# First activation loads of the second stage: issued by GpSimd in five consecutive slots in place of SyncE, pools exchanged two slots earlier

## The chip, the cores and the metric

The kernel runs on one core of a Trainium2 chip. Its time is the device time of one execution in microseconds (us), as the median of several runs. The engines are TensorE (PE, with its weight loads as PEld), VectorE (DVE), ScalarE (ACT), GpSimd (POOL) and SyncE (SP, which only issues DMAs); 16 DMA engines move data between HBM and the on-chip memory.

## The reference

Three parts follow each other, all in float32:

```
a    = softmax(phi over s)                    # B=8, H=8, S=576, D=64, 32 memory slots
k_m, v_m = a^T k, a^T v                       # per batch and head
attn = softmax(q k_m^T / 8) v_m               # -> x: 4608 tokens x 512
x = (h * sigmoid(1.702 h)) @ w_out            # h = x @ w_in, 512 -> 2048 -> 512
x = (h * sigmoid(h)) @ w_out2                 # h = x @ w_in2, the same sizes
```

## The kernel before

Each matmul operand is held as a high part in fp32r and the rest, and a product is three passes (high x high, high x rest, rest x high). The work has three stretches that matter here.

**First stage** (to about 350 us): attention and the first layer's h with its silu. It is a row of N1 = 128 slots. In each, `first` (L372, run twice, u = 0 and 1) makes two blocks of h, 12 matmuls in all (L382), in four PSUM banks that go round, and ACT writes the silu of each (L384) into one half of a tile g. Then `store` (L386) sends the tile, 288 KB, to the scratch tensors g1s in HBM. A tile is named here by its slot, 1 to 128. `g_tile` (L366) gives its buffer: four go round under the tag g, and from tile 117 on, two of three tiles take the buffers raw and wst1, of which there is one each:

```
        if n > TAIL and n % 3:
            return moe.tile([128, 2, HS], F32, tag=("", "raw", "wst1")[n % 3], name="g")
```

Tiles 118, 121, 124 and 127 thus share raw, and 119, 122, 125 and 128 share wst1. Raw belonged to a piece of the first layer's second weight matrix before, which is stored to w1t (L434).

**Second stage** (`middle`, 350 to 700 us): the product of g1s with the first layer's second weights, by Strassen's scheme with seven products of blocks. Its activations come back from g1s by `b_fetch` (L726): 128x2x384 floats, 384 KB, a DMA; a call makes one DMA (tiles named r, in the pool xst) or two (both halves of a tile named rr, in the pool xp). `b_prep` (L751) makes the matmul operand op from such a tile: ACT casts it (L759), DVE takes the rest (L455). `b_prod` (L774) runs 12 matmuls (L780) on it. The first eight loads (the first five entries of the list BF) feed the first eight operands; the other eight of the first block, and twelve loads of weights from w1t, are issued by SyncE at the start of `middle`.

**What sets the order.** The first stage's order is written out: `put(x, fn, ...)` books a step at place x, with three places in a slot (two halves of `first`, one `store`), and a loop runs them in order; every engine then executes its own instructions in that order. SyncE issues every DMA, stores and loads alike, one after the other: an issue that waits holds up all behind it. `swap_pools` (L1025) gives back the memory of the attention (pool att and its PSUM banks) and opens xst and xp in it, from which the loads take their tiles. The first operands are made by `b_make`, booked in slots N1 - 3 and N1 - 2 (operands 0 and 1) and at the start of `middle` (2 and 3).

Of the kernel before, what the change touches and what calls it, by code (L numbers as in the profile page):

```python
# [21 lines left out]
def attn_moe_moe(ctx: ExitStack, tc: tile.TileContext, q, k, v, phi, w1i, w1o, w2i, w2o, out):  # L22
    nc = tc.nc
# [28 lines left out]
    g1s = [dram.tile([128, 2, NT], F32, name=f"g1s{f}") for f in range(NP)]  # L52
# [388 lines left out]
    HB = 384  # L441
# [281 lines left out]
    rb, ob, eb = {}, {}, {}  # L723
    TB = HB // 128

    def b_fetch(b, q, p):  # L726


        if q == 2 or (q == 0 and p < 2):
            x = p if q else 5 + p  # L730
            ts = {p: pools["xst"].tile([128, 2, HB], F32, tag=f"xr{x}", name="r")}
        else:
            i = {0: (0, 6), 1: (5, 7), 3: (3, 4)}[q][p // 2]
            t = pools["xp"].tile([128, 2, 2, HB], F32, tag=f"x{i}", name="rr")
            ts = {p + n: t[:, n] for n in range(2)}
        c0 = (2 * b + q // 2) * HB
        for p, t in ts.items():
            rb[b, q, p] = t
            nc.sync.dma_start(out=t, in_=g1s[4 * (q % 2) + p][:, :, c0:c0 + HB])

    def b_fetch_after(b, i, p):

        for q in {3: (0, 1), 7: (2,), 4: (3,)}.get(i, ()):
            if q == 2 or (q == 0 and p < 2):
                b_fetch(b, q, p)
            elif p % 2:
                b_fetch(b, q, p - 1)
# [118 lines left out]
    def put(x, fn, *a):  # L866

        todo.setdefault(x, []).append((fn, a))
# [11 lines left out]
    def plan_attention(b, z):  # L880
# [29 lines left out]
        for c in range(4):  # L910
            for x, fn, a in zip(t["wp"][c], (wp_mm, wp_hi, wp_lo), ((), (COPY[t["on"][2][c]],), ())):
# [14 lines left out]
                q=(-37, -37, -36, -34, -29, -28), qe=(-37, -34, -34, -29, -29, -28),  # L926
# [5 lines left out]
                q=(-49, -43, -42, -36, -36, -32), qe=(-43, -39, -32, -34, -34, -32),  # L932
# [5 lines left out]
                q=(-43, -41, -40, -37, -36, -32), qe=(-40, -40, -35, -33, -30, -30),  # L938
# [5 lines left out]
                q=(-42, -41, -41, -40, -36, -36), qe=(-42, -40, -36, -33, -31, -31),  # L944
# [75 lines left out]
            for x, fn in zip(WO["sum"][n], (wo1_sum, wo1_hi, wo1_lo, wo1_tail)):  # L1020
                put(66 + 66 * c + x, fn, c, n)
    N1 = 2 * B * NP
    ZS = N1 - 12

    def swap_pools():  # L1025
        att.release()
# [4 lines left out]

    put(3 * ZS + 2, swap_pools)
    BF = [(0, 0), (0, 1), (0, 2), (1, 0), (1, 2), (2, 0), (3, 0), (2, 1), (2, 2), (3, 2), (2, 3)]
    for n, z in enumerate((1, 3, 5, 7, 9)):
        put(3 * (ZS + z) + 2, b_fetch, 0, *BF[n])
    seqb = [(b, i, p) for b in range(NBK) for i in ORDER for p in range(4)]
    AHEAD = 3
    SUMS = {5: ((0, 0),), 6: ((0, 1), (1, 0), (1, 1)), 7: ((2, 0),), 8: ((2, 1), (3, 0)), 9: ((3, 1),)}
# [208 lines left out]
```

## Time and profile before

| | |
|---|---|
| time, median of 3 runs | 1408.13 us (1405.4 to 1409.28) |
| the profiled execution: its own time | 1412.43 us |
| its span | 1410.6 us |
| TensorE busy | 1377.0 us, 98% |
| VectorE, ScalarE, GpSimd busy | 71%, 57%, 22% |
| mean granted clock of TensorE | 0.996 |

The span runs from the first to the last instruction of the profiled execution; its own time has 1.8 us around it. Busy shares are over the whole span, so they say nothing on a single stretch: what a change at one place is worth is read from the rows of that place. A DMA's issue (SyncE, written SPq) is short; how long the transfer then takes is its landing time, listed apart.

### The profile page before, as it was taken

Reading aid. Unit: us, or ns where it says so; the run is one execution under the profiler, and the core shown is the slowest. Engines: PE = TensorE matmul, PEld = TensorE weight load, DVE = VectorE, ACT = ScalarE, POOL = GpSimd, SP = SyncE. Lnnn points to the kernel's source line nnn. Section 1 sums busy time; section 2 is a strip of 40 time slices with the busy share of each in tenths; the row PEclk is TensorE's granted clock in tenths of the full one; section 3 lists DMA queues with packets and bytes.
Section 4 is the critical chain, followed back from the end, with each engine's and each line's share of the span. In section 5 each row is a group of like instructions: output and inputs, shape, how many; then the busy total and the mean of one; then the engine's idle time right before and its main releaser. Section 6 shows DMA issues by size and latency. Waiting matters only on the chain.

```text
span 1410.6 us, 25823 instructions
## 1 busy us (share of the span) xinstructions
PE 1377.0 (98%) x10058; PEld 1322.9 (94%) x10058; DVE 1003.3 (71%) x1328; ACT 797.5 (57%) x1353; POOL 308.1 (22%) x213
## 2 busy tenths in 40 slices
PE   6899999999999999999999999999999999999998
PEld 4687888788999999999999999999999999999998
DVE  6776676663887778888876344343669988898886
ACT  3767777675454555555566566565775444444442
POOL 1524655642000111200000010010000405135050
PEclk9999999999999999999999999999999999999999
DMA  9797888768965572653355664645574643716531
GB/s 360 241 293 243 296 274 299 264 213 260 340 239 165 182 255 93 239 175 127 112 164 190 202 214 154 210 160 196 181 238 140 191 131 105 210 42 185 138 98 34
DMA packets 217722, 276.95 MB, mean 196 GB/s; under 512 B 50688, under 2 KB 198144, under 8 KB 217600
## 3 DMA queue, kind: packets, MB, share of 16 engines
q1 hardware_dynamic: 217600, 275.31, 59.7%
q8 instruction: 79, 1.29, 0.4%
q14 instruction: 43, 0.35, 0.1%
HBM read 166.20 MB, written 109.05 MB: 195 GB/s over the span
## 4 chain that ended last, share of the span: by engine, by line
PE 92%; ACT 2%; DVE 1%; DMA 1%; issue 0%; POOL 0%; DVEq 0%; ACTq 0%; POOLq 0%
PE pb L780 25%; PE p L679 25%; PE xb L564 14%; PE h L382 13%; PE y L564 11%; PE a L334 2%; PE a L247 1%; PE a L208 1%; DMA phi<-in_phi_dram 1%; ACT L384 1%; PE a L270 1%; ACT phi L186 0%; DMA g1s<-g 0%; ACT g L384 0%; DVE slab L345 0%
## 5 line engine op out<-in xcount | busy, mean ns | idle before, releaser
L780 PE MATMUL pb<-op,wq 128*128 128x384 f32 x2016 | 350.4, 335 | 0.0
L780 PEld LDWEIGHTS pb<-op,wq 128*128 128x128 f32 x2016 | 349.7, 188 | 0.6 <-DVE op L455 0.6
L679 PE MATMUL p<-op,wq 128*128 128x384 f32 x2016 | 350.1, 335 | 0.0
L679 PEld LDWEIGHTS p<-op,wq 128*128 128x128 f32 x2016 | 349.7, 188 | 0.2 <-DVE op L455 0.2
L455 DVE TENSOR_TENSOR op<-rr,op 128x768 fp32r<-128x768 f32 x204 | 235.0, 1161 | 52.3 <-ACT op L664 26.8
L382 PEld LDWEIGHTS h<-attnT,slab 128*128 128x128 f32 x1536 | 209.1, 189 | 40.9 <-ACT g L384 16.3
L382 PE MATMUL h<-attnT,slab 128*128 128x288 f32 x1536 | 231.6, 303 | 10.2 <-ACT g L384 7.0
L564 PE MATMUL xb<-xq,wq 128*128 128x384 f32 x1152 | 218.2, 338 | 0.0
L564 PEld LDWEIGHTS xb<-xq,wq 128*128 128x128 f32 x1152 | 203.1, 188 | 0.2
L859 POOL TENSOR_TENSOR c<-c 128x512 int32<-128x512 int32 x32 | 51.3, 1603 | 614.5 <-DVE c L857 522.9
L455 DVE TENSOR_TENSOR op<-r,op 128x768 fp32r<-128x768 f32 x132 | 145.5, 1110 | 54.2 <-ACT op L759 41.2
L564 PE MATMUL y<-xq,wq 128*128 128x384 f32 x864 | 167.5, 338 | 0.1
L564 PEld LDWEIGHTS y<-xq,wq 128*128 128x128 f32 x864 | 152.6, 188 | 0.5 <-ACT e L624 0.5
L664 ACT CAST op<-rr 128x768 fp32r<-128x768 f32 x108 | 89.6, 837 | 97.5 <-PE p L679 70.8
L384 ACT ACTIVATE g<-h 128x288 f32<-128x288 f32 x256 | 98.7, 416 | 79.4 <-PE h L382 53.4
L573 ACT ACTIVATE gq<-e 128x384 f32<-128x384 f32 x144 | 75.6, 525 | 103.2 <-DVE e L452 103.0
L759 ACT CAST op<-rr 128x768 fp32r<-128x768 f32 x96 | 80.0, 835 | 70.5 <-PE pb L780 43.6
L452 DVE TENSOR_TENSOR e<-e,y 128x384 f32<-128x384 f32 x96 | 52.8, 553 | 63.2 <-PE y L564 57.0
L759 ACT CAST op<-r 128x768 fp32r<-128x768 f32 x72 | 60.1, 836 | 50.1 <-PE pb L780 39.2
L452 DVE TENSOR_TENSOR e<-e,xb 128x384 f32<-128x384 f32 x48 | 26.5, 553 | 80.0 <-ACT c L852 37.8
L664 ACT CAST op<-r 128x768 fp32r<-128x768 f32 x60 | 50.3, 838 | 56.4 <-PE p L679 45.5
L452 POOL TENSOR_TENSOR r<-r 128x768 f32<-128x768 f32 x10 | 22.6, 2281 | 271.7 <-DMA out_dram<-ox 117.7
(112 smaller groups left out, 1410.9 us busy)
## 6 DMA issues: line engine op xcount, KB each, us to landing
g1s<-g SPq DMA_DIRECT2D x128, 288.0 KB, 4.2
gs<-gq SPq DMA_DIRECT2D x192, 192.0 KB, 1.9
rr<-g1s SPq DMA_DIRECT2D x60, 384.0 KB, 6.7
rr<-gs SPq DMA_DIRECT2D x60, 384.0 KB, 5.0
r<-g1s SPq DMA_DIRECT2D x36, 384.0 KB, 4.2
r<-gs SPq DMA_DIRECT2D x36, 384.0 KB, 5.6
q<-in_q_dram SPq DMA_DIRECT2D x16, 576.0 KB, 5.4
xs<-eb SPq DMA_DIRECT2D x24, 384.0 KB, 4.2
```

Source lines behind the costliest of these rows:

```text
L334: nc.tensor.matmul(out=a[u][j:j + 32], lhsT=st["kvT", b][r, s, 1, 32 * m:32 * m + 32], rhs=w1[r, m, cols(c)], start=True, stop=True)
L382: nc.tensor.matmul(out=h, lhsT=w[:, wi, g, f0:f0 + 128], rhs=x[:, xi, g * HS:(g + 1) * HS], start=(g == 0 and n == 0), stop=(g == 1 and n ...
L384: nc.scalar.activation(out=t[:, u], in_=h, func=ACTF.Silu, scale=1.702)
L452: eng.tensor_tensor(out=out, in0=a, in1=b, op=ALU.add)
L455: eng.tensor_tensor(out=out, in0=a, in1=b, op=ALU.subtract)
L564: nc.tensor.matmul(out=out, lhsT=w[:, s, wi, f0:f0 + 128], rhs=x[:, s, xi], start=(start and s == 0 and k == 0), stop=(s == 1 and k == 2), ...
L573: nc.scalar.activation(out=t, in_=h, func=ACTF.Silu, scale=2.0)
L664: nc.scalar.copy(out=t[:, :, 0], in_=s)
L679: nc.tensor.matmul(out=out[:, d], lhsT=w[:, u, wi, d * 128:(d + 1) * 128], rhs=t[:, u, gi], start=(start and p == 0 and u == 0 and k == 0) ...
L759: nc.scalar.copy(out=t[:, :, 0], in_=s)
L780: nc.tensor.matmul(out=out[:, d, :HB], lhsT=w[:, u, wi, d * 128:(d + 1) * 128], rhs=t[:, u, gi], start=(start and p == 0 and u == 0 and n ...
L859: nc.gpsimd.tensor_tensor(out=i, in0=i, in1=low, op=ALU.add)
```

## The change

Five calls of `b_fetch`, eight DMAs, are booked with nc.gpsimd as issuer, in slots ZS + 1 to ZS + 5 (in place of every second slot from ZS + 1 to ZS + 9), and ZS, the slot of `swap_pools`, is N1 - 14 in place of N1 - 12. Other calls of `b_fetch` keep SyncE.

```
-    def b_fetch(b, q, p):
+    def b_fetch(b, q, p, by=nc.sync):
...
-            nc.sync.dma_start(out=t, in_=g1s[4 * (q % 2) + p][:, :, c0:c0 + HB])
+            by.dma_start(out=t, in_=g1s[4 * (q % 2) + p][:, :, c0:c0 + HB])
...
-    ZS = N1 - 12
+    ZS = N1 - 14
...
-    for n, z in enumerate((1, 3, 5, 7, 9)):
-        put(3 * (ZS + z) + 2, b_fetch, 0, *BF[n])
+    for n, z in enumerate((1, 2, 3, 4, 5)):
+        put(3 * (ZS + z) + 2, b_fetch, 0, *BF[n], nc.gpsimd)
```

On SyncE, at the stores of tiles 116 to 121, before (L388 is a store of g, L739 a load; the number behind g1s is the eighth of the scratch, that behind _ the buffer):

```order
L388 DMA g1s3_87<-g_4837 256x1x288
L388 DMA g1s4_88<-g_4855 256x1x288
L739 DMA r_4901<-g1s0_84 128x2x384
L388 DMA g1s5_89<-g_4884 256x1x288
L388 DMA g1s6_90<-g_4904 256x1x288
L739 DMA r_4940<-g1s1_85 128x2x384
L388 DMA g1s7_91<-g_4922 256x1x288
L388 DMA g1s0_84<-g_4943 256x1x288
L739 DMA rr_4978<-g1s2_86 128x2x384
L739 DMA rr_4978<-g1s3_87 128x2x384
```

Two stores, one call's loads, two stores, and so on to the end of the stage. On SyncE at the end of the stage, now:

```order
L388 DMA g1s5_89<-g_5045 256x1x288
L388 DMA g1s6_90<-g_5066 256x1x288
L388 DMA g1s7_91<-g_5084 256x1x288
L739 DMA r_5114<-g1s0_84 128x2x384
L739 DMA rr_5116<-g1s4_88 128x2x384
L739 DMA rr_5116<-g1s5_89 128x2x384
L739 DMA r_5119<-g1s1_85 128x2x384
```

The stores follow each other up to tile 128, and the first loads on SyncE are those that `middle` issues. On GpSimd, from its last sum over the weights (L455) to its next work in the second stage (L859), now:

```order
L455 TENSOR_TENSOR wq_4812<-wst1_4083,wq_4812 128x2x256
L739 DMA r_4865<-g1s0_84 128x2x384
L739 DMA r_4885<-g1s1_85 128x2x384
L739 DMA rr_4905<-g1s2_86 128x2x384
L739 DMA rr_4905<-g1s3_87 128x2x384
L739 DMA rr_4926<-g1s4_88 128x2x384
L739 DMA rr_4926<-g1s5_89 128x2x384
L739 DMA rr_4948<-g1s6_90 128x2x384
L739 DMA rr_4948<-g1s7_91 128x2x384
L859 TENSOR_TENSOR c2_5411<-c2_5411 128x512 x16
```

The eight loads stand in one row there, between L455 and L859, which followed each other before.

## Rows read from the trace of the kernel before

**Rows 1.** The page: TensorE's part of the engine table, and the chain.

```profile
PE 1377.0 (98%) x10058; PEld 1322.9 (94%) x10058; DVE 1003.3 (71%) x1328; ACT 797.5 (57%) x1353; POOL 308.1 (22%) x213
...
PE 92%; ACT 2%; DVE 1%; DMA 1%; issue 0%; POOL 0%; DVEq 0%; ACTq 0%; POOLq 0%
```

**Rows 2.** Stretches: length, busy us (x instructions) of PE, PEld, DVE, ACT, POOL; clock, DMA share, GB/s.

```profile
328.00:330.00 2.00, 1.98 (x13) 1.58 (x12) 2.00 (x4) 0.82 (x2) 0.03 (x1) 1.00 0.68 242
330.00:340.00 10.00, 10.00 (x76) 10.00 (x76) 0.92 (x1) 4.90 (x13) 0.00 (x0) 1.00 0.84 266
340.00:351.00 11.00, 9.29 (x69) 9.06 (x68) 1.92 (x2) 4.75 (x12) 0.00 (x0) 1.00 1.02 303
351.00:360.00 9.00, 9.00 (x54) 9.00 (x53) 3.74 (x5) 5.78 (x11) 0.00 (x0) 1.00 0.98 329
```

**Rows 3.** Order of time on PE: start, us, work [idle before <- what ended it].

```profile
320.35 1.95 PE L334 MATMUL a<-w,kvT 64*32 64x512 f32 x32
...
347.08 3.46 PE L382 MATMUL h<-attnT,slab 128*128 128x288 f32 x24 [1.71 <-ACT g L384]
350.38 15.81 PE L780 MATMUL pb<-op,wq 128*128 128x384 f32 x88
```

**Rows 4.** Chain that ended last, in order of time: start, us, what.

```profile
340.65 5.86 DMA g1s<-g
```

**Rows 5.** Order of time on ACT, 331 to 360 us.

```profile
331.87 0.41 ACT L384 ACTIVATE g<-h 128x288 f32<-128x288 f32 x1 [0.44 <-PE h L382]
332.62 0.41 ACT L384 ACTIVATE g<-h 128x288 f32<-128x288 f32 x1 [0.34 <-PE h L382]
...
335.81 0.41 ACT L384 ACTIVATE g<-h 128x288 f32<-128x288 f32 x1 [0.39 <-PE h L382]
337.98 1.51 ACT L384 ACTIVATE g<-h 128x288 f32<-128x288 f32 x4 [1.75 <-DMA g1s<-g]
...
342.56 0.71 ACT L384 ACTIVATE g<-h 128x288 f32<-128x288 f32 x2 [1.53 <-DMA g1s<-g]
346.62 0.71 ACT L384 ACTIVATE g<-h 128x288 f32<-128x288 f32 x2 [3.35 <-DMA g1s<-g]
...
359.68 0.83 ACT L759 CAST op<-rr 128x768 fp32r<-128x768 f32 x1
```

**Rows 6.** Order of time on SyncE (issues, merged where equal ones follow each other).

```profile
328.38 0.56 SPq L434 DMA_DIRECT2D w1t<-wq  x1
...
332.07 1.43 SPq L739 DMA_DIRECT2D r<-g1s  x1
333.59 1.58 SPq L388 DMA_DIRECT2D g1s<-g  x2
...
339.32 1.24 SPq L739 DMA_DIRECT2D rr<-g1s  x2
340.65 1.27 SPq L388 DMA_DIRECT2D g1s<-g  x2
```

**Rows 7.** POOL: order of time, and one line of its costliest groups (busy, mean ns).

```profile
326.73 1.30 POOL L455 TENSOR_TENSOR wq<-wst,wq 128x512 fp32r<-128x512 f32 x1 [0.21 <-ACT wq L513]
403.51 1.30 POOL L859 TENSOR_TENSOR c<-c 128x512 int32<-128x512 int32 x1 [75.48 <-DVE c L857]
...
L455 POOL TENSOR_TENSOR rr<-rr 128x768 f32<-128x768 f32 x10 | 25.4, 2560 | 0.0
```

**Rows 8.** Landing (median us): stores 300-330, 330-341; w1t store at 328.38; g1s, 318-352.

```profile
g1s<-g SPq DMA_DIRECT2D x15, 288.0 KB, 2.7
...
g1s<-g SPq DMA_DIRECT2D x6, 288.0 KB, 4.2
...
w1t<-wq SPq DMA_DIRECT2D x1, 512.0 KB, 3.3
...
DMA to landing us min/median/max: 2.5/5.4/6.9
```

**Rows 9.** Order of time on DVE: its first operand of the second stage.

```profile
348.09 0.96 DVE L455 TENSOR_TENSOR op<-r,op 128x768 fp32r<-128x768 f32 x1 [17.17 <-ACT op L759]
```

## The prediction

> **What bounds the kernel now.** I read the page's table of engines and its chain first, then the busy time by stretch around the place of the change, then the order of time on TensorE, ScalarE, SyncE, GpSimd and VectorE there. TensorE (PE) is the bound: 98% busy, and 92% of the chain that ended last lies on it [rows 1]. A change to who issues loads can therefore only pay where PE stands still because of the loads. The stretch table shows how much that is: in 330 to 340 us and from 351 to 360 PE is busy all the time, in 340 to 351 it is busy for 9.29 of 11 us, while the share of the DMA engines goes from 0.84 to 1.02 [rows 2]. PE's own list has one gap there, 1.71 us in front of the last 24 first-stage matmuls, ended by the silu of L384 on ScalarE (ACT) [rows 3]. So **1.71 us, 0.12% of the span, is all that this place has to give**.
>
> Why ACT was late is read from the chain in order of time: a store of g that takes 5.86 us stands between ACT and PE [rows 4]. It stands there because of g_tile (L366): from tile 117 on, two tiles of three use one buffer for each of the tags raw and wst1, so tile n of those cannot be written before the store of tile n - 3 has landed. Counted back from the last store (tile 128), ACT's waits [rows 5] are: tile 121 waits 1.75 us for store 118, tile 124 waits 1.53 for store 121, tile 125 waits 3.35 for store 122. The four h banks in PSUM let PE run two tiles ahead, so only the third of these reaches PE. SyncE's list shows a second cause beside the landing: tile 122 was done at 339.49 (337.98 + 1.51, the last of four silus), but its store was issued at 340.65, behind two of the moved loads that held SyncE from 339.32; tile 118, done at 333.03, was issued at 333.59, behind the first moved load, which took 1.43 us [rows 5, 6].
>
> **The change part by part.** *Eight loads leave SyncE.* Five calls of b_fetch are eight DMAs of 384 KB. No store of this stretch stands behind a load any more, so a store goes out when its second silu ends: 0.56 us earlier for tile 118, 1.16 for tile 122. Nothing new takes the place on SyncE. What follows the last store there, the second batch of loads, starts as soon as that store is issued, so no later than now.
>
> *Eight issues come to GpSimd (POOL).* Its last instruction before them is L455, from 326.73 to 328.03, and its next one starts at 403.51 [rows 7]; for 75 us nothing is queued behind the loads. They wait only for matmuls of the attention that lie before 322.3 (the L334 group ends there [rows 3]), so the first goes out at about 328.0, against 332.07 now. No row shows a DMA issued by POOL. The nearest rows are SyncE's issues of the same loads, 1.43 us for the first and 0.62 each for the two at 339.32 [rows 6], and POOL's own pass over a tile of the same size, 2.56 us [rows 7]. The issues are hidden at both ends: at 2.56 the last one starts at 328.03 + 7 x 2.56 = 345.9; with the longest landing of this stretch, 6.9 us [rows 8], it is there at 352.8, and ACT first reads it at 359.68 [rows 5]. I take SyncE's rows as the nearer ones and cost this at nothing. VectorE (DVE) has work until 330.92 and then none until 348.09 [rows 9].
>
> The Trainium skill (SBUF — State Buffer, section SBUF: two separate sides, the box on DVE blocking DMA) speaks against this part: GpSimd writes the descriptors of its DMAs into SBUF and cannot while VectorE holds the port pair that they share, where DMAs from SyncE are immune. By it a load could lose at most VectorE's busy time; the trace leaves 2.9 us of that at the start and none after, so the sum would stay. No run here shows yet whether the lock acts.
>
> *The transfers move forward and together.* The bytes are the same. Before, eight loads were spread over 332 to 350; now they are asked for from 328 on. The room for them is in 328 to 340, where the DMA share was 0.68 and 0.84, and not in 340 to 351, where it was 1.02 [rows 2]. That is good for the late stores and bad for the early ones. The price goes by the landing time L of a store. After a landing ACT needs 0.11 us (340.65 + 5.86 = 346.51 against 346.62 [rows 4, 5]); I use 0.15. Tile 118 is ready at 333.03. Tile 121 starts at 333.05 + L + 0.15 and lasts 0.72; tile 124 starts L + 0.15 after the store of 121, and its first half takes 0.41. That half is done at 334.5 + 2L. PE needs it for tile 126, whose first matmul would start at 343.75: PE came to rest at 345.37 (347.08 - 1.71 [rows 3]) after finishing tile 126, and one tile takes 1.60 (tiles 118 and 120 end on ACT at 333.03 and 336.22 [rows 5]). So **PE stalls 2 x (L - 4.6) us**, nothing below L = 4.6, and as much as now, 1.71, at L = 5.45. The other chain (119, 122, 125), with tile 119 ready at 334.62, gives 336.1 + 2L against 345.35, the same point.
>
> L is bounded by rows: 2.7 us median with little other traffic, 4.2 in 330 to 341, 5.86 for the store that made the gap, 6.9 the longest [rows 4, 8]. I take 4.2, since the new overlap of stores and loads falls into that stretch, and the traffic taken out of 341 to 351 lies where 5.86 was. One more thing is due early: tile 118 takes over the buffer of the last w1t store, issued at 328.38 and landing in 3.3 us [rows 6, 8], just before the tile's first silu at 331.87 [rows 5]. That store has 512 KB, 1.6 us of data at the 329 GB/s of a full stretch [rows 2]; if loads beside it double that, tile 118 ends at 328.38 + 4.9 + 0.15 + 0.72 = 334.15 in place of 333.03 and puts 1.1 us on the chain. With L = 4.2 the slack is 0.8, so a stall of 0.3 us remains.
>
> *The swap of the pools* two slots earlier leaves the order of the work on PE, ACT and DVE as it is and puts no wait there but those for the loads themselves; it lies behind the last matmul into the released banks and costs nothing.
>
> Sum: -1.71 + 0.3 = **-1.4 us**. Against the profiled execution (1412.43 us, span 1410.6) that is 1411.0; against the median of the runs, 1408.13, it is **1406.7 us**. From 351 to 360 PE has no idle time [rows 2]; the second batch of loads starts no later and finds less queued before it, so I count nothing there.
>
> **The rivals.** *The stores lose to the bunched loads* (the one on the other side). POOL asks for 3.1 MB within eight issues, while a store of 288 KB comes each 1.60 us, on the same DMA engines. If L goes to 6.9 in 333 to 344, the stall is 2 x 2.3 = 4.6 us, 2.9 more than now: 1411.0. It decides from L = 5.45. For it: a store right behind two loads took 5.86 [rows 4], and the w1t store is now hit too. Against it: the loads lie over a stretch with a share of 0.84, stores no longer stand behind them on SyncE, and a late tile delays the next store and so thins the traffic. Between 1408.1 and 1411.0, chance 0.32.
>
> The Trainium skill (DMA: Bandwidth & Descriptors, section Issuing engines are not separate DMA queues) has a rule near this rival: DMAs of all issuers end on the same 16 engines, and a second issuer saves only issue time. By that alone, with each landing as now, tile 125's first half would be done at 339.45 + 5.86 + 0.15 + 0.41 = 345.87, a stall of 0.5 us, and the time 1406.9. The trace agrees in that the DMA share was already 1.02.
>
> *POOL's issues are slow, so that the change doesn't bring the loads early.* Then PE waits for op at L780. The eighth load feeds the eighth product; a product is 12 matmuls, 12 x 15.81/88 = 2.16 us [rows 3], so its operand is due at 350.38 + 7 x 2.16 = 365.5, and its cast and subtraction (0.83 + 0.96 [rows 5, 9]) begin by 363.7. An issue may take (363.7 - 6.9 - 328.03)/7 = 4.1 us before anything is late. At 5 us the load lands at 369.9 and PE loses 6 us: 1414. For it: the trace has no such issue. Against it: the nearby rows are at 2.56 or below, and DVE is idle. Chance 0.06.
>
> *The stall was this execution's own*: the other runs did not have it, and the time stays at 1408.1. For it: there is one profile, and the three runs lie 3.9 us apart. Against it: the waits follow from buffers and sizes that are the same each time. Chance 0.10.
>
> **How the numbers follow.** The forecast, L below 5, has 0.52. Its likeliest time is 1406.7, and its own range is 1404.4 (a gain of all 1.71 less half of the spread of the runs) to 1407.5 (a stall of 1.1 us). The range for 8 in 10 takes in the rival of the bunched loads and the same spread below: 1403.8 to 1411.3. A measurement of this kernel can tell about 0.3%, 4.2 us, from no change. Nothing in the forecast reaches that, since 1.71 us is all there is; 0.05 for faster is the drift of medians alone. Slower by over 4.2 us needs L above 7.5 in the second case, or the third case: 0.03 + 0.05 = 0.08. Within: 0.87.
>
> **What would show it.** In the profile after, POOL should hold eight issues from 328 on, each below 2.6 us, and SyncE nothing but stores from there to about 351. The stores should land within 5 us, ACT's three waits, 6.6 us together [rows 5], should fall below 3, and PE's gap before the last h matmuls should be gone or below 0.5. The first product of L780 would start near 348.9. If stores land in 5.5 us or more, or tile 118 starts after 333, the second case holds; if ACT's casts of L759 wait for loads, the third. A fall by 5 us or more, or a new gap after 360, would mean that something outside these stretches changed, which the order of the program does not show.

## The result and the profile after

The changed kernel takes 1417.61 us (median of 6 runs, 1414.82 to 1419.01), the kernel before 1409.01 on the same chip (6 runs); the ratio is **1.0054, with a 95% interval from 1.0039 to 1.0069**. By that ratio it is slower by 7.6 us (5.5 to 9.7); the two medians are 8.6 us apart. Forecast were 1406.7 us, a range of 1403.8 to 1411.3 and no measurable change, so the prediction was wrong, in sign and in range.

The profiled execution of the change took 1415.07 us. Two profiles of different executions differ by some us in places that the change doesn't touch (below), so they are compared by one stretch: from the end of the last L334 group, ahead of the change, to the first matmul of the second stage, L780. Before, it was 322.30 to 350.38, 28.1 us [rows 3]. PE's order of time after:

```profile
317.48 1.06 PE L334 MATMUL a<-w,kvT 64*32 64x512 f32 x16
318.47 11.95 PE L382 MATMUL h<-attnT,slab 128*128 128x288 f32 x84
331.88 5.06 PE L382 MATMUL h<-attnT,slab 128*128 128x288 f32 x36 [1.46 <-ACT g L384]
341.56 11.36 PE L382 MATMUL h<-attnT,slab 128*128 128x288 f32 x72 [4.63 <-ACT g L384]
352.76 27.47 PE L780 MATMUL pb<-op,wq 128*128 128x384 f32 x157
```

From 318.54 to 352.76 it is 34.2 us, 6.1 more. Where 1.71 us of idle time stood, there are two gaps, 1.46 and 4.63 us; that is 4.4 more. The rest is behind the second gap: the last 72 matmuls of h are six tiles, 9.6 us at the 1.60 of [rows 5], and take 11.2 (341.56 to 352.76). The stretch tables show why (columns as in [rows 2]), first by the stretches of before, then by 2 us:

```profile
330.00:340.00 10.00, 5.47 (x40) 5.00 (x38) 0.00 (x0) 2.14 (x6) 0.13 (x1) 1.00 1.04 393
340.00:351.00 11.00, 9.44 (x59) 9.44 (x60) 1.04 (x2) 6.17 (x15) 0.00 (x0) 0.84 0.42 147
...
342.00:344.00 2.00, 2.00 (x11) 2.00 (x10) 0.00 (x0) 1.02 (x3) 0.00 (x0) 0.54 0.51 174
344.00:346.00 2.00, 2.00 (x12) 2.00 (x11) 0.00 (x0) 0.59 (x2) 0.00 (x0) 0.61 0.36 126
346.00:348.00 2.00, 2.00 (x17) 2.00 (x17) 0.00 (x0) 1.05 (x3) 0.00 (x0) 1.00 0.40 143
```

Behind 4.63 us of idle time PE's granted clock is 0.54 and 0.61, near the lower of its two levels (1.2 of 2.4 GHz), before it is back at 1.00: 11 and 12 matmul records in 2 us in place of 17. Before, the clock was 1.00 across the 1.71 us gap [rows 2]. So 4.4 + 1.6 = 6.0 of the 6.1 us are accounted for.

The other half of the picture is the DMA share: 1.04 at 393 GB/s while PE idles in 330 to 340, and 0.42 after it. The same bytes came earlier and all at once. GpSimd's order of time, then the landing of what was issued between 324 and 341 us (median us, last column), and of all DMAs on g1s between 318 and 352:

```profile
322.97 1.30 POOL L455 TENSOR_TENSOR wq<-wst,wq 128x512 fp32r<-128x512 f32 x1 [0.18 <-ACT wq L513]
324.21 1.60 POOL L739 DMA_DIRECT2D r<-g1s  x2
325.81 4.32 POOL L739 DMA_DIRECT2D rr<-g1s  x6
405.40 1.29 POOL L859 TENSOR_TENSOR c<-c 128x512 int32<-128x512 int32 x1 [75.27 <-DVE c L857]
```

```profile
rr<-g1s POOLq DMA_DIRECT2D x6, 384.0 KB, 9.6
g1s<-g SPq DMA_DIRECT2D x6, 288.0 KB, 8.9
r<-g1s POOLq DMA_DIRECT2D x2, 384.0 KB, 6.9
w1t<-wq SPq DMA_DIRECT2D x1, 512.0 KB, 6.7
...
DMA to landing us min/median/max: 2.5/6.1/11.3
```

Eight loads go out in 5.9 us, 0.72 to 0.87 us each, since GpSimd has nothing else to do and waits for nothing. That is 3.15 MB, or 530 GB/s asked for, beside the stores. A store lands in 8.9 us where it took 4.2 in [rows 8], the w1t store in 6.7 where it took 3.3. These two waits are the chain (start, us, what), and ScalarE's two long waits:

```profile
324.62 6.69 DMA w1t<-wq
...
332.15 8.84 DMA g1s<-g
```

```profile
331.41 1.32 ACT L384 ACTIVATE g<-h 128x288 f32<-128x288 f32 x4 [3.74 <-DMA w1t<-wq]
...
341.10 1.51 ACT L384 ACTIVATE g<-h 128x288 f32<-128x288 f32 x4 [6.91 <-DMA g1s<-g]
```

The first is tile 118, which takes over the buffer that w1t is stored from; the second is tile 121, which waits for store 118. Behind the stretch these two profiles hardly differ: from L780 to the end it is 1410.6 - 350.38 = 1060.2 us before and 1413.3 - 352.76 = 1060.5 after.

### The profile page after: what moved, and what is told of

The parts are those of the page before. It is cut to its first block, busy times and chain, and to the rows that moved or that the text cites. A ratio compares the mean times of both kernels' runs of the same rounds, so it can differ in the third digit from the quotient of the medians.

```text
span 1413.3 us, 25826 instructions
## 1 busy us (share of the span) xinstructions
PE 1378.3 (98%) x10058; PEld 1324.1 (94%) x10058; DVE 1001.6 (71%) x1328; ACT 798.4 (56%) x1353; POOL 313.5 (22%) x221
## 3 DMA queue, kind: packets, MB, share of 16 engines
q0 software_dynamic: 896, 3.15, 0.6%
## 4 chain that ended last, share of the span: by engine, by line
PE 88%; DMA 3%; DVE 2%; ACT 2%; issue 1%; POOL 0%; SPq 0%; DVEq 0%; ACTq 0%; POOLq 0%
PE pb L780 25%; PE p L679 23%; PE xb L564 14%; PE h L382 11%; PE y L564 11%; PE a L334 2%; DVE op L455 1%; PE a L247 1%; DMA phi<-in_phi_dram 1%; PE a L208 1%; DMA g1s<-g 1%; PE a L270 0%; DMA w1t<-wq 0%; ACT L384 0%; DMA rawe<-in_moe_w_out_dram 0%
## 5 line engine op out<-in xcount | busy, mean ns | idle before, releaser
L780 PE MATMUL pb<-op,wq 128*128 128x384 f32 x2016 | 350.0, 335 | 0.0
L780 PEld LDWEIGHTS pb<-op,wq 128*128 128x128 f32 x2016 | 349.8, 188 | 0.0
L455 DVE TENSOR_TENSOR op<-rr,op 128x768 fp32r<-128x768 f32 x204 | 237.2, 1172 | 50.4 <-ACT op L664 26.4
L564 PE MATMUL xb<-xq,wq 128*128 128x384 f32 x1152 | 218.2, 338 | 0.0
L564 PEld LDWEIGHTS xb<-xq,wq 128*128 128x128 f32 x1152 | 203.2, 188 | 0.2
L859 POOL TENSOR_TENSOR c<-c 128x512 int32<-128x512 int32 x32 | 51.5, 1611 | 614.1 <-DVE c L857 510.1
L455 DVE TENSOR_TENSOR op<-r,op 128x768 fp32r<-128x768 f32 x132 | 144.4, 1102 | 60.7 <-ACT op L759 48.0
L564 PE MATMUL y<-xq,wq 128*128 128x384 f32 x864 | 167.5, 338 | 0.1
L564 PEld LDWEIGHTS y<-xq,wq 128*128 128x128 f32 x864 | 152.7, 188 | 0.5 <-ACT e L624 0.5
L759 ACT CAST op<-rr 128x768 fp32r<-128x768 f32 x96 | 80.0, 835 | 70.0 <-PE pb L780 41.6
L759 ACT CAST op<-r 128x768 fp32r<-128x768 f32 x72 | 60.1, 835 | 50.6 <-PE pb L780 42.9
L452 DVE TENSOR_TENSOR e<-e,xb 128x384 f32<-128x384 f32 x48 | 26.5, 553 | 79.9 <-ACT c L852 37.8
```

The costliest lines, as they stand in the source:

```text
L452: eng.tensor_tensor(out=out, in0=a, in1=b, op=ALU.add)
L455: eng.tensor_tensor(out=out, in0=a, in1=b, op=ALU.subtract)
L564: nc.tensor.matmul(out=out, lhsT=w[:, s, wi, f0:f0 + 128], rhs=x[:, s, xi], start=(start and s == 0 and k == 0), stop=(s == 1 and k == 2), ...
L759: nc.scalar.copy(out=t[:, :, 0], in_=s)
L780: nc.tensor.matmul(out=out[:, d, :HB], lhsT=w[:, u, wi, d * 128:(d + 1) * 128], rhs=t[:, u, gi], start=(start and p == 0 and u == 0 and n ...
L859: nc.gpsimd.tensor_tensor(out=i, in0=i, in1=low, op=ALU.add)
```

## The experiments

**Theories.** A: the loads are asked for faster than the DMA engines serve them, whoever issues them; the stores queue behind, and the reuse of a g buffer after three slots carries that to PE. B: GpSimd's queue beside SyncE's is what hurts. C: the earlier swap hurts. D: the loss lies elsewhere. One thing needs no run: with GpSimd as issuer, the slots of before and the slots of the change give the same program. Built from both sources, the order on every engine, waits included, is the same row for row, since nothing else stands on GpSimd in these slots. So the change's slot numbers and its earlier swap do nothing, and pace nothing; what counts is the issuer alone. On SyncE the stores between the loads had paced them.

All ratios are against the kernel before on the same chip, whose median was 1409.0 us with the change and 1410.0 to 1410.2 with the others; "stretch" is the one defined above, from each kernel's one profile. "Gaps" are PE's idle times of over 0.3 us in it and, behind a +, in the first products of L780.

| run | issuer, density of the eight loads | stretch | gaps | median | ratio (95%) |
|---|---|---|---|---|---|
| before | SyncE, every second slot | 28.1 | 1.71 | 1409.0 | 1 |
| the change | GpSimd, 5.9 us | 34.2 | 1.46, 4.63 | 1417.6 | 1.0054 (1.0039 to 1.0069) |
| sync_bunch | SyncE, 6.0 us | 34.3 | 6.38 | 1416.1 | 1.0048 (1.0029 to 1.0066) |
| sync_n14 | SyncE, five slots in a row | 30.2 | 2.18, 0.97 | 1412.9 | 1.0019 (1.0008 to 1.0030) |
| paced_n14 | GpSimd paced, five slots in a row | 31.6 | 0.80, 2.68 | 1409.4 | 0.9994 (0.9982 to 1.0006) |
| pool_paced | GpSimd paced, every second slot | 26.5 | 0 + 0.33, 0.55 | 1406.6 | 0.9981 (0.9969 to 0.9994) |
| paced_again | the same kernel | 27.6 | 1.25 + 0.46 | 1406.7 | 0.9984 (0.9969 to 1.0000) |
| act_n12 | ScalarE, every second slot | 26.9 | 0.49 + 1.71, 0.55 | 1410.6 | 1.0000 (0.9985 to 1.0014) |
| after_ring6 | the change, g in a ring of six | 27.9 | 1.50 | 1409.8 | 0.9997 (0.9987 to 1.0007) |
| after_ring6b | the same, raw reused later | 27.4 | 0.68 | 1409.8 | 0.9996 (0.9985 to 1.0007) |
| before_ring6 | before, g in a ring of six | 26.1 | 0 | 1407.8 | 0.9979 (0.9967 to 0.9992) |
| paced_ring6 | GpSimd paced, and ring of six | 26.1 | 0 + 0.87 | 1404.4 | 0.9965 (0.9952 to 0.9979) |

### Is it the issuer, or the burst?

**sync_bunch**: all eight loads on SyncE in one row.

```
+    ZS = N1 - 14
+    for n, z in enumerate((1, 1, 1, 1, 1)):
+        put(3 * (ZS + z) + 2, b_fetch, 0, *BF[n])
```

> The earlier swap, and all eight loads issued by SyncE in one row behind the store of tile 115, the densest that SyncE can do. SyncE needs about 0.6 us an issue, so eight take 5 us, as with GpSimd. Theory A (the burst is what hurts, whoever issues it): the stores behind it land 8 us or more after their tiles are ready, PE stalls 5 to 7 us before the second stage, time 5 to 9 us over before, like the change. Theory B in its weak form (GpSimd's queue takes more than its share of the DMA engines, and that makes half of the loss): 2 to 4 us over before, as with SyncE in five slots.

SyncE's and PE's order of time, and the stretch table:

```profile
327.16 1.59 SPq L739 DMA_DIRECT2D r<-g1s  x2
328.84 4.30 SPq L739 DMA_DIRECT2D rr<-g1s  x6
333.36 22.49 SPq L388 DMA_DIRECT2D g1s<-g  x13
```

```profile
343.47 11.38 PE L382 MATMUL h<-attnT,slab 128*128 128x288 f32 x72 [6.38 <-ACT g L384]
354.69 9.60 PE L780 MATMUL pb<-op,wq 128*128 128x384 f32 x54
```

```profile
340.00:351.00 11.00, 7.53 (x45) 7.53 (x46) 0.00 (x0) 4.39 (x11) 0.00 (x0) 0.69 0.58 200
```

SyncE issues the eight in 6.0 us, PE has one gap of 6.38 us, the clock falls with it (0.69 in 340 to 351), and the ratio is 1.0048, the loss of the change. GpSimd is not needed for it: the gap and the time are those of theory A, and above the 2 to 4 us of B's weak form.

The loss is not made up in the same way, though. The chain has the store of tile 118:

```profile
335.40 7.50 DMA g1s<-g
```

ScalarE was done with that tile at 331.14 us. Its store went out 4.3 us later, behind the row of loads on SyncE, and then took 7.50 us to land. In the change the store went out at once and took 8.84. So here a part of the delay is the wait for SyncE itself, and this run alone does not show that a store beside GpSimd's loads fares no worse; pool_paced (below) bears on that.

**sync_n14**: the change with SyncE as the issuer (slots 1 to 5, no other edit).

> The slots and the earlier swap of the change, but SyncE as the issuer: between two stores stands one call of b_fetch, in five slots in a row. Theory A (the loads are asked for faster than the DMA engines can serve, whoever issues): 3.1 MB of loads and five stores within 8 us against about 365 GB/s leave 1.7 MB queued, stores land in about 7 us, PE stalls 4 to 6 us, time 2 to 5 us over before. Theory B (what hurts is GpSimd's queue standing beside SyncE's): within 1.5 us of before. Theory C (the earlier swap hurts by itself): as slow as the change, +8 us.

```profile
338.29 1.86 PE L382 MATMUL h<-attnT,slab 128*128 128x288 f32 x12 [2.18 <-ACT g L384]
341.12 3.45 PE L382 MATMUL h<-attnT,slab 128*128 128x288 f32 x24 [0.97 <-ACT g L384]
344.75 5.06 PE L382 MATMUL h<-attnT,slab 128*128 128x288 f32 x36 [0.17 <-ACT g L384]
```

The gaps sum to 3.3 us, the ratio is 1.0019. With one store between two calls, the five calls take 9.3 us to issue (326.17 to 335.45) in place of 5.9, and about two thirds of the loss are gone. The time is what A expected at this density; the stall came out below its 4 to 6 us. C falls: the same swap, with a third of the loss.

### Pacing GpSimd

**pool_paced**: GpSimd in the slots of before; ahead of each call it copies one column of the slot's tile, and so waits for its silu.

```
-    ZS = N1 - 14
+    ZS = N1 - 12
...
-    for n, z in enumerate((1, 2, 3, 4, 5)):
+    for n, z in enumerate((1, 3, 5, 7, 9)):
...
+        if by is nc.gpsimd:
+            nc.gpsimd.tensor_copy(out=pacer, in_=st["g"][2][:, 1, 0:1])
```

> GpSimd issues the eight loads, in the slots of before (N1 - 12, every second slot), and ahead of each call it copies one column of that slot's g tile, so that it waits for the silu of the slot and cannot run ahead. Theory A: the loads come as they did before, stores land in 4 to 6 us, time within 2 us of before, or up to 1.7 us below it. Theory B: with GpSimd's queue beside SyncE's the stores still land in 8 us or more behind a pair of loads, PE stalls 4 us or more, time 4 to 8 us over before.

GpSimd's order of time (L742 is L739 of the change, by three added lines), and PE's:

```profile
336.71 0.18 POOL L739 COPY pacer<-g 128x1 f32<-128x1 f32 x1 [2.15 <-ACT g L385]
337.15 1.45 POOL L742 DMA_DIRECT2D rr<-g1s  x2 [0.27 <-issue]
340.84 0.18 POOL L739 COPY pacer<-g 128x1 f32<-128x1 f32 x1 [2.24 <-ACT g L385]
341.28 1.45 POOL L742 DMA_DIRECT2D rr<-g1s  x2 [0.27 <-issue]
```

```profile
319.25 26.69 PE L383 MATMUL h<-attnT,slab 128*128 128x288 f32 x192
```

A copy of 0.18 us restores the spacing; 192 matmuls of h, all 16 tiles, run without a gap, and the kernel is 2.7 us faster than before by the ratio (0.9981). Paced, GpSimd as the issuer costs nothing; B falls. How much of the gain comes from the stretch is less clear: it is 1.6 us shorter, of which 0.9 come back as gaps in the first products.

**paced_n14**: the same pacing, in the slots of the change.

> GpSimd's paced loads, but in the slots of the change: N1 - 14 and five slots in a row, one call behind each silu. Theory A in its sharper form (what counts is how many loads are asked for per slot): two loads and a store a slot, 1.06 MB in 1.6 us, are more than the DMA engines serve, so stores land in 7 us or more, PE stalls 3 to 5 us, and the time is 1 to 4 us over before, as with SyncE in these slots. If it is enough that GpSimd cannot run ahead of the slots: as the paced kernel in the slots of before, 2 to 3 us under before.

```profile
337.95 1.85 PE L383 MATMUL h<-attnT,slab 128*128 128x288 f32 x12 [0.80 <-ACT g L385]
342.48 9.76 PE L383 MATMUL h<-attnT,slab 128*128 128x288 f32 x60 [2.68 <-ACT g L385]
```

In the stretch the sharper form of A holds: 3.5 us of gaps, as with SyncE at this density. The time does not follow: 0.9994, where the stretch, 31.6 us, is 3.5 longer than before. What it gains lies behind the stretch (1407.7 - 352.08 = 1055.6 us to the end). So this run supports A by its trace and not by its time.

**act_n12**: ScalarE issues, in the slots of before (nc.scalar for nc.gpsimd).

> The eight loads issued by ScalarE in the slots of before, so that they leave SyncE's row but are paced by ScalarE's own silus. Theory A: no store waits behind a load's issue and the loads are not bunched; stores land in 4 to 5 us, PE's gap falls from 1.71 us to below 1, time 0 to 1.7 us below before. If a second queue by itself takes the stores' share: stores land in 7 us or more, and the time is 2 us or more over before.

```profile
351.57 0.44 PE L780 MATMUL pb<-op,wq 128*128 128x384 f32 x1 [1.71 <-ACT op L759]
352.57 9.66 PE L780 MATMUL pb<-op,wq 128*128 128x384 f32 x46 [0.55 <-DVE op L455]
```

The gap of h falls to 0.49 us as expected, but two gaps of 1.71 and 0.55 come in the first products of L780, because ScalarE's casts for them stand behind its silus, which wait for the last stores. The ratio is 1.0000 (0.9985 to 1.0014). For the time this is inconclusive; in the stretch a gain of 1.2 us is given back by the later waits. They also cost clock: 0.55 and 0.59 in 352 to 356, right behind the two gaps, and 1.00 again from 356. From L780 to the end it is 1064.0 us, 3.8 more than before.

### The channel: the ring of g buffers

**after_ring6**: the change, with the six buffers in turn from tile 118 on, so that a store has six slots to land in place of three.

```
-        if n > TAIL and n % 3:
-            return moe.tile([128, 2, HS], F32, tag=("", "raw", "wst1")[n % 3], name="g")
+        if n > TAIL and (n - 118) % 6 < 2:
+            return moe.tile([128, 2, HS], F32, tag=("raw", "wst1")[(n - 118) % 6], name="g")
```

> The changed kernel, with the buffers of g from tile 118 on in a ring of six (raw, wst1 and the four of g in turn) in place of reusing raw and wst1 each third tile. If the loss goes through the reuse of a g buffer after three slots, as theories A and B both have it, a landing of 9 us is covered by six slots (9.6 us): the 4.63 us gap and the drop of the clock behind it go, the 1.46 us gap at tile 118 (behind the w1t store) stays, and the time is 5 to 8 us below the changed kernel, within 2 us of before. Theory D (the loss lies elsewhere, outside the ring): the time stays at that of the change.

```profile
333.52 14.66 PE L382 MATMUL h<-attnT,slab 128*128 128x288 f32 x108 [1.50 <-ACT g L384]
```

The burst is still there (stores land in 6.7 us, median of 316 to 340), the 4.63 us gap is gone, the one at tile 118 stays, and the time is back at that of before, some 8 us below the change. This is the channel, and D falls: against the kernel before, no loss that can be measured lies elsewhere.

**after_ring6b**: the ring begins with wst1 at tile 119 and raw at tile 120 (`(n - 119) % 6 < 2`, tags in that order).

> The changed kernel with the same ring of six, whose first use of raw is now tile 120 in place of tile 118, two slots after the last w1t store out of raw. The gap of 1.50 us at tile 118 that the first ring of six kept was that store's landing: it goes, PE has no gap before the second stage, and the time is 1 to 2 us below that of the first ring of six, 1408 to 1409, though the eight loads still go out within 6 us and stores still take 9 us or more to land. If the gaps at this place are not the whole loss, the time stays at that of the first ring of six or above.

The gap at tile 118 goes as expected, but a gap of 0.68 us comes later, in front of the last three tiles, and the time is not lower than with the first ring (1409.8 both). That part of the expectation failed: with no early gap, the tiles run into the late landings instead (11.20 us for the store of tile 118, on the chain up to that gap).

**before_ring6**: the kernel before, with this ring.

> The kernel before, with the ring of six buffers for g from tile 119 on (wst1, raw, then the four of g), so that a store has six slots to land. If PE's 1.71 us gap of before comes from the three-slot reuse alone, it goes, and the time falls by about 1.7 us (ratio 0.9988). If the gap was that one execution's own, the time stays (ratio 1.0000).

```profile
320.85 26.35 PE L382 MATMUL h<-attnT,slab 128*128 128x288 f32 x192
```

No gap, and 0.9979 (0.9967 to 0.9992): the 1.71 us of before came from the three-slot reuse, and the longer ring removes them without moving a load. This run also puts after_ring6b in its place: with the same ring, the change takes 1409.8 us and the kernel before 1407.8, and the stretch is 27.4 and 26.1. The ring hides most of what the burst costs; it does not make the burst free.

**paced_ring6**: both remedies.

> GpSimd's paced loads in the slots of before, together with the ring of six. The paced kernel had no gap before the second stage, but 0.9 us of gaps in the first products of L780, since ScalarE waited for stores of the last tiles ahead of its casts. With six slots to land those waits go too: 0.5 to 1 us below the paced kernel, ratio to before about 0.9975. If the two remedies remove the same gap, the same time as the paced kernel.

It is the fastest, 1404.4 us, ratio 0.9965 (0.9952 to 0.9979; 5 runs), 13 us below the change. A new gap of 0.87 us stands in the first products of L780 all the same, behind DVE, which waited 4.1 us for a load of the second batch while the DMA share was 1.03 to 1.07 (346 to 364). By stretch and gaps this kernel is 0.4 and 1.1 us better than the two profiles of the paced kernel; the rest of the 2.2 us between their medians is not explained by this place.

### What two profiles of one kernel differ by

**before_again**, **after_again** and **paced_again** are the two kernels and pool_paced once more.

> The kernel before once more, for a second profile. If the parts of the span outside the change are steady, the last L334 group ends at 322.3 us, the second stage starts 28.1 us later, and from there to the end it is 1060.2 us, each within 0.5 us. If single executions differ outside the change, these parts move by 1 to 4 us while the 28.1 stays near.

> The changed kernel once more, for a second profile. The stretch from the end of the last L334 group to the first L780 was 34.2 us, with two gaps on PE and a drop of the clock; if this is what the change costs, it is 33.5 to 36 us again, and the stretches ahead of it and behind it differ between the two profiles as they do for the kernel before.

> The paced kernel (GpSimd, slots of before, a copy of one column ahead of each call) once more. From its stretch between the last L334 group and the first products, 0.7 us shorter than before, its time should be 0.7 us below before; measured was 2.7 below, with 4 us less in the third stage, L565. If that third stage is a matter of the execution, the time comes out 0.5 to 2 us below before this time; if it belongs to the kernel, 2.5 us or more below, with 334 ns a matmul in L565 again.

PE's order of time in the second profile of before, then of the change:

```profile
317.31 1.95 PE L334 MATMUL a<-w,kvT 64*32 64x512 f32 x32
319.19 23.14 PE L382 MATMUL h<-attnT,slab 128*128 128x288 f32 x168
343.28 3.46 PE L382 MATMUL h<-attnT,slab 128*128 128x288 f32 x24 [0.95 <-ACT g L384]
346.58 17.75 PE L780 MATMUL pb<-op,wq 128*128 128x384 f32 x101
```

```profile
332.40 5.06 PE L382 MATMUL h<-attnT,slab 128*128 128x288 f32 x36 [1.20 <-ACT g L384]
341.48 12.38 PE L382 MATMUL h<-attnT,slab 128*128 128x288 f32 x72 [4.02 <-ACT g L384]
353.69 10.64 PE L780 MATMUL pb<-op,wq 128*128 128x384 f32 x60
```

The stretch is 27.3 us for before (28.1 the first time) and 34.4 for the change (34.2), so its cost is 6 to 7 us in each pairing, which agrees with the 7.6 of the ratio (5.5 to 9.7). The other parts move more, and alike in both kernels: the L334 group of before ends at 319.26 and not at 322.30, and the way from L780 to the end is 1056.5 us and not 1060.2 (for the change 1056.8 and not 1060.5). A page line on L564, the third stage's matmuls of xb, shows where most of the latter lies; first before, then its second profile, then paced_again:

```profile
L564 PE MATMUL xb<-xq,wq 128*128 128x384 f32 x1152 | 218.2, 338 | 0.0
```

```profile
L564 PE MATMUL xb<-xq,wq 128*128 128x384 f32 x1152 | 215.9, 336 | 0.0
```

```profile
L565 PE MATMUL xb<-xq,wq 128*128 128x384 f32 x1152 | 215.9, 334 | 0.0
```

One kernel has 218.2 us in one execution and 215.9 in another, so this is a matter of the execution. All four profiles of paced kernels are at the low value, and their times are 2 to 4 us lower than their stretches and gaps explain. Whether the pacing copy has a part in that stays open: paced_again came out at 0.9984 (0.9969 to 1.0000), 2.3 us below before, between the two cases of its expectation.

## Why the prediction was wrong

- **The source of the 1.71 us was right, and as a bound on this place it held.** before_ring6 removes the gap by buffers alone, shortens the stretch by 2.0 us, the gap and 0.3 us more, and gains 0.21% (0.08 to 0.33); pool_paced, whose loads leave SyncE, has no gap ahead of the second stage in its first profile (1.25 us in its second) and gains 0.19% (0.06 to 0.31). 1.71 us is 0.12%, within both intervals. paced_ring6 gains more than that, 0.35% (0.21 to 0.48), with a stretch no shorter than that of before_ring6; what it gains beyond the bound lies elsewhere, and its cause stays open.
- **GpSimd's part was right in its terms and wrong in its meaning.** The first issue follows L455 at once (324.21; L455 ends at 324.27), an issue takes 0.72 to 0.87 us, within the bound of 2.56, and no cast of L759 waits for the eight loads, so the third rival is out. The rule on VectorE holding back GpSimd's descriptors, cited from the Trainium skill (SBUF — State Buffer, section SBUF: two separate sides), played no part that shows: VectorE was busy up to 327.15 us, and the issues that began by then took 0.87, 0.73, 0.72 and 0.72 us, against 0.72 for those after it. Whether VectorE's work of that time holds the ports at all, no row shows. But the quick issue was booked as harmless. That nothing was queued behind the loads on GpSimd also means that nothing spaced them.
- **The step that failed is the term L**, the landing time of a store, taken as 4.2 us and bounded at 6.9 by rows of before. All those rows had the loads spaced by stores on one queue; none was a bound for eight at once. The numbers for a better one stood in the text: 3.1 MB in eight issues. From the trace after, as an estimate: from 324.0 to 332.15 us, when store 118 goes out, 3.15 MB of loads, 0.52 of w1t and 0.9 of three stores are asked for. The table by 2 us has 218, 150, 405 and 394 GB/s there, so 2.3 MB of them are served and 2.2 MB wait. At the 393 GB/s of 330 to 340 that is 5.7 us, and with the 2.5 us that a store takes alone in this profile store 118 needs some 8 us. Measured were 8.84 for it, the store that made the gap, and a median of 8.9.
- **The formula 2 x (L - 4.6) was of the wrong regime.** It counts two late landings in a row. With L at 8.8, tile 121 alone stops PE (4.63 us), during which no store is issued and the burst drains; the next store lands in 2.5 us. So the loss is less than 2 x 4.2, and it came with a second price that the sum did not have at all, 1.6 us (2.6 in the second profile) of lower clock behind the gap.
- **The w1t store was seen and undersized**: 4.9 us were put for its landing, 6.69 were measured, and it made a gap of its own, 1.46 us.
- **The rival of the bunched loads was the right mechanism**, with 0.32 and a price of at most 1411.0, since its L stopped at 6.9 as well. Its argument against itself, that late tiles thin the traffic, holds for the stores and not for the loads, which wait for nothing. The rule that was cited with it, from the Trainium skill (DMA: Bandwidth & Descriptors, section Issuing engines are not separate DMA queues), is borne out: sync_bunch and the change ask for the same bytes in the same time from two issuers and lose the same. What was drawn from it, each landing as now, was not; nor does a row show the 339.45 us that it starts from (rows 5 give 339.49 for tile 122), on which nothing hangs.
- **"The stall was this execution's own"** is out: the second profile of before has it too, with 0.95 us.

## What to carry to other kernels

Moving loads to an idle queue removes not only the issue time from the busy one but also the spacing that the busy one gave them; what then paces them has to be named, and if it is nothing, the bytes over the time of their issues are to be set against what the DMA engines serve. A landing time read from a trace is a price for the spacing in that trace. Where a buffer is reused after n slots, n slots' time is the landing that it covers; here lengthening that ring gained as much as moving and pacing the loads (0.21% and 0.19%), and without touching the traffic.

## What was not expected of the hardware

A DMA that GpSimd issues occupies it for 0.72 to 0.87 us for 384 KB, close to SyncE's 0.6 us, and the page counts its packets as fewer and larger. The queue line of the page of the change, software_dynamic being GpSimd's:

```profile
q0 software_dynamic: 896, 3.15, 0.6%
```

That is 896 packets for 3.15 MB, 3.5 KB each, where SyncE's queue has 217,600 packets for 275.31 MB in the kernel before, 1.3 KB each. With paced loads no effect of this on the stores was seen: over the 13 stores of tiles 116 to 128 the median landing is 5.0 and 4.9 us with GpSimd (pool_paced, paced_again), 5.4 and 4.8 with SyncE (before, before_again). For the burst it is open: the stores of tiles 116 to 120 took 8.4 to 10.6 us in the change and 7.0 to 8.0 in sync_bunch, but there they went out only behind all eight loads.

PE's granted clock after idle time: at 1.00 through gaps of 1.71 us (before), of 2.18 and 0.97 (sync_n14) and 1.50 (after_ring6); 0.84 in 340 to 351 after 0.80 and 2.68 us in paced_n14; about half behind 4.63 (the change) and with 6.38 (sync_bunch), but also behind 1.71 and 0.55 us with a single matmul between them (act_n12, 0.55 and 0.59 in 352 to 356). So the length of one gap does not settle it. In the second profile of the change, behind 4.02 us:

```profile
342.00:344.00 2.00, 2.00 (x10) 2.00 (x9) 0.00 (x0) 1.12 (x3) 0.00 (x0) 0.50 0.45 157
344.00:346.00 2.00, 2.00 (x11) 2.00 (x10) 0.00 (x0) 0.41 (x1) 0.00 (x0) 0.50 0.42 147
```

Where the clock falls, a gap so has a second price, 1.6 to 2.6 us in the two profiles of the change, on the matmuls that come after it.
